# Attention and two feed-forward blocks on one core: zero products of 512 columns, feature rows by transfers, value sums on GpSimd, two heads' values in split halves

## The chip, the core and the metric

One core of a Trainium2 chip runs the whole program. TensorE multiplies, VectorE and ScalarE work on what it leaves in PSUM and on SBUF, GpSimd and SyncE issue most transfers. The metric is the device time of one execution in microseconds, as a median of several runs. One execution is also taken by the hardware profiler, and all rows below come from it.

## The reference

Bucketed attention, then two feed-forward blocks, all in float32. With 2 x 8 heads, 768 positions and 64 features:

```python
q_bits = (np.einsum('bhsd,dk->bhsk', q, proj) > 0)      # 6 bits; the same for k
mask = q_bucket[:, :, :, None] == k_bucket[:, :, None, :]
scores = np.where(mask, scale * q @ k.T, -1e9)
attn = exp(scores - max); attn = attn / (sum + 1e-9)
x = attn @ v                                            # (1536, 512)
h = x @ w_in; g = h * tanh(softplus(h)); x = g @ w_out  # d_ff 2048
h = (x @ w1) * (x @ w2) @ w3; out = h @ w_out2          # d_ff 1024
```

## The kernel before, in words

**A head.** Head u's q and k are loaded (L411), split into a rounded half and the rest for one-pass products (`hlqk`, L400 and L432), transposed on TensorE (L441) and copied to `qb` and `kb` by ScalarE (L447). Products with `psel` (L472) give the projections, and VectorE compares them with zero (L479); the resulting bits are 12 extra feature rows of `qa` and `ka`, whose other 64 rows are copies from `qb` and `kb` (L400; the 12 rows of `ka` are copied at L484). From head 2 on, a further operand `xf` is filled by two transfers on SyncE's queue (L456).

A head has six rows of scores, of 128 positions by 768. A row is four products into a score tile `s` (L499; two such tiles exist, `s_67` and `s_68`, and transposes and projections use them too), a maximum on VectorE (L508) and an exponential on ScalarE into `E` (L511). For each half of three rows, six groups of three transposes (L545) bring `E` to PSUM, a copy takes each to SBUF as `T` (L400, on ScalarE or VectorE), and three groups of two products (L569) multiply `T` with the values `v`. These are full float32 products of 64 output rows, and the trace shows each as two records. The groups end with a copy and an add into `X` (L577, L590). Two more columns of `T`, holding 1/768, yield the mean of the values, which L596 adds up. The row sums' reciprocals go through a transpose (L528) and a transfer to memory.

**Weights.** GpSimd issues the loads (L622). The weights are decoded in one ScalarE and three VectorE instructions (L606, L609, L612, L615), and split into halves where they are used (L661 and L663); L694 to L720 multiply w3 by w_out2 beforehand, which is wprod in the code. The first block of 512 tokens passes the feed-forward part among the later heads (L775, L791, L886), the other two blocks follow from about 523 us on (L775, L1133, L1160, L1188).

**What sets the order.** No loop does. Every piece is a unit with an engine, a cost, a due time and what it reads and writes; `Plan.run` simulates the engines with these costs and the latencies in `LAT`, and lets each engine take whichever unit can start first, the earlier due time deciding. The result is one fixed instruction order for each engine, in which an instruction waits for everything ahead of it. `CFG` holds the numbers that set due times (in rows of scores) and pool sizes. After that, `Plan.fill` puts zero products (L392, results never read) into TensorE's order wherever the plan has a gap in its first 60 us:

```python
n = int((b - a - 0.15) / 0.06)
...
nc.tensor.matmul(t[:, 0:128], lhsT=zr, rhs=zr, start=True, stop=True)
```

Of the kernel before, what the change touches and what calls it, by code (L numbers as in the profile page):

```python
# [26 lines left out]
CFG = {  # L27
    "lag": 1.18,
    "prep": 8.06,
    "wp0": 16.01,  # L30
    "wp1": 51.97,
    "dec0": 47.99,
    "dec1": 88.63,
    "ff0": 56.0,
    "ff1": 102.69,
# [7 lines left out]
    "tc": 22,  # L43
# [39 lines left out]
class Plan:  # L83
    LAT = {"PE": 0.22, "DVE": 0.17, "ACT": 0.17, "POOL": 0.3, "SP": 2.3, "SWAP": 0.0}
# [202 lines left out]
def kernel(  # L287
# [68 lines left out]
    TP = mkpool("T", 7, [128, HS + 2], pa)  # L356
# [7 lines left out]
    VP = mkpool("v", 4, [128, C, D], pa)  # L364
    TM = mkpool("tm", 2, [D, HS + 2], pa)
# [54 lines left out]

    def prep(u, d0, step):
# [5 lines left out]
        for x, (nm, hi, fb) in enumerate((("q", 0, qb), ("k", 1, kb))):  # L427
# [16 lines left out]
            P.op("PE", 6 * 0.082, tr, r=[hl], w=[t], due=d(x + 1), name=f"tq{u}")  # L444
# [8 lines left out]
        if u > 1:  # L453
            xf = Val(XF, "x")
            for sl, fb, nm in ((slice(0, D), qb, "q"), (slice(D, 2 * D), kb, "k")):
                P.op("SP", 0.5, lambda sl=sl, fb=fb: nc.sync.dma_start(  # L456
                    out=xf()[sl].bitcast(F32), in_=fb()[sl].bitcast(F32)), r=[fb], w=[(xf, nm)], due=d(2.5), lat=2.0, name=f"xf{u}")
        P.op(EITHER, (act(S, True), dve2(S)), lambda e: copy(e, qa()[0:D], qb()[0:D]),
             r=[qb], w=[(qa, "x")], due=d(2.2), name=f"fa{u}")
        P.op(EITHER, (act(S, True), dve2(S)), lambda e: copy(e, ka()[0:D], kb()[D:2 * D]),  # L460
             r=[kb], w=[(ka, "x")], due=d(3.2), name=f"fa{u}")
# [16 lines left out]
        def cmp():  # L478
# [5 lines left out]
        P.op("DVE", dve2(S), lambda: nc.vector.tensor_copy(out=ka()[D:KR], in_=qa()[96:96 + 2 * NB]),  # L484
             r=[(qa, "m")], w=[(ka, "m")], due=d(4.6), name=f"km{u}")
# [4 lines left out]
    v_mvs, v_rd = Val(), Val()  # L490
# [25 lines left out]
    def norm(u, due):  # L516
# [3 lines left out]
        def sc():  # L520
# [7 lines left out]
        P.op("PE", 0.16, lambda: nc.tensor.transpose(t()[0:C, 0:128], s()[:, 3], ident), r=[(s, 3)], w=[t],  # L528
             due=due + 0.5, name=f"nt{u}")
# [4 lines left out]
            r=[rt], w=[(v_rd, (u, ))], due=due + 0.7, lat=2.2, name=f"rd{u}")  # L534
# [4 lines left out]
    def unit(u, a, kt, due):  # L539
# [9 lines left out]
        f = et[u, a, kt] = Val(TP, "T")  # L549

        def cp(eng):
            copy(eng, f()[:, 0:HS], t()[:, 0:HS])

        if CFG["tc"] > n0_of(u, a):
            eng, cost = ("ACT",), (act(HS) + 0.02,)
        else:
            eng, cost = EITHER, (act(HS) + 0.02, dve(HS))
        P.op(eng, cost, (lambda: cp("ACT")) if len(eng) == 1 else cp, r=[t], w=[f], due=due + 0.15, name=f"TC{u}.{a}.{kt}")

    def values(u, a, j, due):  # L560
# [4 lines left out]
        n = HS + 2 if a == 0 else HS  # L565

        def mm():
            for x in range(2):
                nc.tensor.matmul(  # L569
                    t()[x * D:(x + 1) * D, 0:n], lhsT=vs[u]()[:, 2 * j + x, :], rhs=fs[x]()[:, 0:n],  # L570
                    start=(j == 0), stop=(j == CH - 1))

        P.op("PE", 0.93, mm, r=fs + [vs[u]], w=[t], due=due, name=f"V{u}.{a}.{j}")
# [671 lines left out]
```

## Time and profile before

| | |
|---|---|
| median of 3 runs | 838.75 us (838.18 to 839.08) |
| the profiled execution | 839.55 us, of which the span from first to last instruction is 837.8 |
| TensorE busy | 823.1 us, 98% of the span |
| VectorE, ScalarE busy | 551.3 and 465.7 us |
| mean granted clock of TensorE | 0.998 |
| moved by the DMA queues | 118.47 MB |

Busy time is the union of an engine's records; records of neighbouring instructions overlap a little, so means by line add to more. Idle time costs only on the engine that the end waits for. The span runs from a head's start-up (to some 40 us) over the attention heads (the last scores at 491 us) to the two later token blocks.

### The profile page before, as it was taken

To read this page: it belongs to the slowest core of one execution; us is meant where nothing else is said; L and a number is where in the kernel's file an instruction comes from. 1 tells how busy PE (TensorE), PEld (TensorE's weight loads), DVE (VectorE), ACT (ScalarE), POOL (GpSimd) and SP (SyncE) were. 2 spreads that over 40 slices of the span, in tenths; PEclk is the share of its full clock that TensorE was granted. 3 is DMA by queue.
4 is the path that set the end of the run, shared out by engine and by line. 5 is a ranking of instruction groups with operands and counts; after the bars stand their busy time and mean duration, and the time that the engine had idled before them with its cause. 6 is when DMAs were issued, how large, how long until landed. Compare 5 with 4: busy or idle time off the path is not lost.

```text
span 837.8 us, 10922 instructions
## 1 busy us (share of the span) xinstructions
PE 823.1 (98%) x4198; PEld 637.1 (76%) x4198; DVE 551.3 (66%) x782; ACT 465.7 (56%) x735; POOL 42.5 (5%) x84
## 2 busy tenths in 40 slices
PE   9999999999989999999999999999999999999998
PEld 9977777777666766767777777888888888888886
DVE  3489878778889899989997566733644334332412
ACT  3379865666879978877675444633343333342311
POOL 3000000000101111111110000000000000000000
PEclk9999999999999999999999999999999999999999
DMA  7514433333956758667662203933212208300001
GB/s 271 222 36 152 139 112 103 111 92 115 286 178 209 256 176 275 243 217 268 217 205 72 83 6 133 407 125 104 79 69 88 102 1 317 110 26 1 1 0 51
DMA packets 40356, 118.47 MB, mean 141 GB/s; under 512 B 4496, under 2 KB 10992, under 8 KB 39280
## 3 DMA queue, kind: packets, MB, share of 16 engines
q1 hardware_dynamic: 27936, 67.31, 24.3%
q0 software_dynamic: 12224, 50.34, 17.5%
q8 instruction: 33, 0.54, 0.3%
q14 instruction: 19, 0.16, 0.1%
q10 hardware_dynamic: 144, 0.13, 0.0%
HBM read 94.37 MB, written 17.87 MB: 134 GB/s over the span
## 4 chain that ended last, share of the span: by engine, by line
PE 78%; DVE 12%; DMA 4%; issue 3%; ACT 3%; SPq 0%; DVEq 0%; ACTq 0%
PE s L1160 11%; PE b L1133 11%; PE s L775 11%; PE b L791 6%; PE b L569 6%; PE b L886 6%; PE b L1188 5%; PE s L499 5%; PE b L545 5%; PE b L711 4%; PE b L392 4%; DMA f<-r_d 3%; DVE st L508 2%; PE s L472 2%; PE b L775 2%
## 5 line engine op out<-in xcount | busy, mean ns | idle before, releaser
L663 DVE TENSOR_TENSOR k<-f,k 128x1024 fp32r<-128x1024 f32 x96 | 116.0, 1219 | 76.4 <-ACT k L661 76.2
L661 ACT CAST k<-f 128x1024 fp32r<-128x1024 f32 x96 | 99.2, 1047 | 20.5 <-DMA f<-keep_wo 7.8
L511 ACT ACTIVATE E<-s,st 128x768 f32<-128x768 f32 x96 | 86.8, 904 | 41.1 <-DVE st L508 40.0
L508 DVE TENSOR_REDUCE st<-s 128x1 f32<-128x768 f32 x96 | 90.9, 951 | 21.6 <-PE s L499 20.9
L400 ACT COPY T<-b 128x384 f32<-128x384 f32 x129 | 60.4, 483 | 60.1 <-PE b L545 59.8
L545 PE MATMUL b<-ident,E 128*128 128x128 f32 x576 | 93.1, 275 | 0.1
L545 PEld LDWEIGHTS b<-ident,E 128*128 128x128 f32 x576 | 71.0, 140 | 28.6 <-issue 9.0
L1160 PE MATMUL s<-k,k 128*128 128x512 f32 x384 | 91.2, 394 | 0.0
L1133 PE MATMUL b<-k,k 128*128 128x512 f32 x384 | 90.3, 393 | 0.0
L775 PE MATMUL s<-k,k 128*128 128x512 f32 x384 | 89.9, 391 | 0.0
L569 PE MATMUL b<-T,v 128*64 128x386 f32 (+1 forms) x384 | 85.2, 515 | 2.7 <-DVE T L400 2.7
L1160 PEld LDWEIGHTS s<-k,k 128*128 128x128 f32 x384 | 72.1, 188 | 16.8
L1133 PEld LDWEIGHTS b<-k,k 128*128 128x128 f32 x384 | 72.1, 188 | 16.5
L775 PEld LDWEIGHTS s<-k,k 128*128 128x128 f32 x384 | 72.1, 188 | 15.9
L791 PE MATMUL b<-k,k 128*128 128x512 f32 x288 | 81.0, 412 | 1.6 <-DVE k L851 1.6
L791 PEld LDWEIGHTS b<-k,k 128*128 128x128 f32 x288 | 51.3, 191 | 22.2 <-issue 9.6
L1111 ACT ACTIVATE f<-s 128x1024 f32<-128x1024 f32 x16 | 16.4, 1027 | 75.1 <-PE s L775 75.1
L1169 DVE TENSOR_TENSOR f<-s,f 128x512 f32<-128x512 f32 x16 | 11.1, 692 | 69.6 <-ACT f L1168 69.6
L499 PE MATMUL s<-kb,qb 128*128 128x384 f32 x192 | 53.2, 358 | 3.0 <-ACT E L511 2.7
L711 PE MATMUL b<-k,k 128*128 128x512 f32 x192 | 55.3, 413 | 0.0
L775 PE MATMUL b<-k,k 128*128 128x512 f32 x192 | 54.7, 410 | 0.5 <-ACT rt L530 0.5
L886 PE MATMUL b<-k,k 128*128 128x512 f32 x192 | 54.9, 411 | 0.0
(113 smaller groups left out, 1169.2 us busy)
## 6 DMA issues: line engine op xcount, KB each, us to landing
k<-in_moe_w_dram POOLq DMA_DIRECT2D x16, 1024.0 KB, 6.8
k<-in_moe_w_out_dram POOLq DMA_DIRECT2D x12, 1024.0 KB, 8.2
f<-keep_wi SPq DMA_DIRECT2D x24, 512.0 KB, 4.5
f<-keep_wo SPq DMA_DIRECT2D x24, 512.0 KB, 3.4
k<-in_moe_w_in_dram POOLq DMA_DIRECT2D x8, 1024.0 KB, 7.4
f<-keep_wa SPq DMA_DIRECT2D x12, 512.0 KB, 5.8
f<-keep_wb SPq DMA_DIRECT2D x12, 512.0 KB, 7.2
f<-wp_d SPq DMA_DIRECT2D x12, 512.0 KB, 3.7
```

The costliest lines, as they stand in the source:

```text
L499: nc.tensor.matmul(t()[:, a, 0:HS], lhsT=l()[0:kk, i * 128:(i + 1) * 128], rhs=r()[0:kk, a * HS:(a + 1) * HS], start=(l is qb), stop=(l is ...
L508: P.op("DVE", 0.868, lambda: nc.vector.tensor_reduce(out=s()[:, 0, i:i + 1], in_=t()[:, :, 0:HS], axis=AX.XY, op=ALU.max, negate=True), r= ...
L545: nc.tensor.transpose(t()[:, ci * 128:(ci + 1) * 128], es[ci]()[:, kt * 128:(kt + 1) * 128], ident)
L569: nc.tensor.matmul(t()[x * D:(x + 1) * D, 0:n], lhsT=vs[u]()[:, 2 * j + x, :], rhs=fs[x]()[:, 0:n], start=(j == 0), stop=(j == CH - 1))
L661: P.op("ACT", act(1024, True), lambda: nc.scalar.copy(out=hl()[:, 0:1024], in_=f()), r=[f], w=[(hl, 0)], due=due, name="hi")
L663: P.op("DVE", dve(1024), lambda: nc.vector.tensor_sub(out=hl()[:, 1024:2048], in0=f(), in1=hl()[:, 0:1024]), r=[f, (hl, 0)], w=[(hl, 1)], ...
L711: nc.tensor.matmul(acc(), lhsT=hv()[:, ws, g_, :], rhs=wview(wo2[g_ // 2], 2)[:, rs, g_ % 2, :], start=(n == 0), stop=(n == 3 * GT - 1))
L775: nc.tensor.matmul(of(), lhsT=wview(w, KD)[:, ws, kk, (f % 2) * 128:(f % 2) * 128 + 128], rhs=kview(xhl[n][kk // 2], xs, kk), start=(m == ...
L791: nc.tensor.matmul(of(), lhsT=l(), rhs=rr(), start=(m == 0), stop=(m == len(ops) - 1))
L886: nc.tensor.matmul(t(), lhsT=wview(w, KD)[:, ws, kk, f2 * 128:f2 * 128 + 128], rhs=kview(x2[kk // 2], xs, kk), start=(kk == 0 and s == 0), ...
L1133: nc.tensor.matmul(t(), lhsT=wview(w, 2)[:, ws, f, dd * 128:(dd + 1) * 128], rhs=gv[:, gs, f, :], start=(j == 0 and f == 0 and s == 0), st ...
L1160: nc.tensor.matmul(t()[:, x, :], lhsT=wview(w, KD)[:, ws, kk, (f % 2) * 128:(f % 2) * 128 + 128], rhs=kview(xx[kk // 2], xs, kk), start=(k ...
```

## The change

Zero products have 512 columns, read the identity `identr` for both operands, and are counted by 0.43 us each in the plan's first 8 us and by 0.235 after. The 64 feature rows of `qa` and `ka` and the 12 bit rows of `ka` come by transfers on SyncE's queue from head 1 on. GpSimd sums the values of each head over six chunks in three adds, and a product with a column of 1/768 (next to the reciprocals' transpose) takes the mean; the two extra columns of `T` and the adds of L596 go. For heads 3 and 4 the values and `T` are split into halves, so that four one-pass products of 384 columns stand for two full ones. The copies of `T` may be VectorE's from the start. And several numbers that the plan orders by are others, the latencies it assumes too. The line numbers of the changed kernel are some 30 higher (L411 is L415, L508 is L535).

```diff
 CFG = {
-    "lag": 1.18,
-    "prep": 8.06,
-    "wp0": 16.01,
+    "lag": 1.92,
+    "prep": 10.06,
+    "wp0": 20.27,
...
+    "fv0": 3,
+    "fv1": 5,
...
-    LAT = {"PE": 0.22, "DVE": 0.17, "ACT": 0.17, "POOL": 0.3, "SP": 2.3, "SWAP": 0.0}
+    LAT = {"PE": 0.22, "DVE": 0.17, "ACT": 0.17, "POOL": 0.3, "SP": 3.2, "SWAP": 0.0}
...
-            n = int((b - a - 0.15) / 0.06)
-            if n < 4:
+            n = int((b - a - 0.1) / (0.43 if a < CFG["cold"] else 0.235))
+            if n < 1:
...
-            nc.tensor.matmul(t[:, 0:128], lhsT=zr, rhs=zr, start=True, stop=True)
+            nc.tensor.matmul(t.rearrange("p (a n) -> p a n", a=4), lhsT=identr, rhs=identr[:, None, :].to_broadcast([128, 4, 128]),
+                             start=True, stop=True)
...
+            nc.gpsimd.tensor_add(out=o, in0=t()[:, 0:3], in1=t()[:, 3:6])
+            nc.gpsimd.tensor_add(out=o[:, 0], in0=o[:, 0], in1=o[:, 1])
+            nc.gpsimd.tensor_add(out=o[:, 0], in0=o[:, 0], in1=o[:, 2])
+
+        P.op("POOL", 1.3, total, r=[t], w=[m], due=u * C, name=f"vs{u}")
...
+    def feature(u, o, to, f, fr, part, due, name):
+
+        r = [(f, "m")] if part == "m" else [f]
+        if u < 1:
+            P.op(EITHER, (act(S, True), dve2(S)), lambda e: copy(e, o()[to], f()[fr]), r=r, w=[(o, part)], due=due, name=name)
+        else:
+            P.op("SP", 0.5, lambda: nc.sync.dma_start(out=o()[to].bitcast(F32), in_=f()[fr].bitcast(F32)),
+                 r=r, w=[(o, part)], due=due, lat=4.5, name=name)
...
-        P.op("DVE", dve2(S), lambda: nc.vector.tensor_copy(out=ka()[D:KR], in_=qa()[96:96 + 2 * NB]),
-             r=[(qa, "m")], w=[(ka, "m")], due=d(4.6), name=f"km{u}")
+        feature(u, ka, slice(D, KR), qa, slice(96, 96 + 2 * NB), "m", d(4.6), f"km{u}")
...
+            nc.tensor.matmul(t()[rows, 256:258], lhsT=vsum[u]()[:, 0], rhs=mean, start=True, stop=True)
...
+        if u in FRV:
+            P.op("DVE", dve(HS), lambda: nc.vector.tensor_sub(out=f[1](), in0=t()[:, 0:HS], in1=f[0]()), r=[t, f[0]],
+                 w=[f[1]], due=due, name=f"TL{u}.{a}.{kt}")
...
+                if u in FRV:
+                    w = vs[u]()[:, kt * 2 * D:(kt + 1) * 2 * D]
+                    ops += [(slice(0, 128), w, fs[x][s], x + s == 0, x + s == 2) for s in range(2)]
+                else:
+                    ops.append((rows, vs[u]()[:, kt], fs[x][0], True, True))
```

**Where the order moves: TensorE's start.** The first rows of TensorE's order before, up to the transposes of head 0's two halves (`hlqk`); `crow` holds the constants that VectorE copies to `ccol`.

```order
L392 MATMUL b_70<-zr 128x128 x25
L966 MATMUL b_69<-ident,crow 128x128 x2
L392 MATMUL b_70<-zr 128x128 x28
L441 MATMUL s_67<-identr,hlqk_102 128x128 x6
L441 MATMUL s_68<-identr,hlqk_103 128x128 x6
L392 MATMUL b_69<-zr 128x128 x6
```

The same place in the changed kernel, where the constants stand in `f_154`:

```order
L395 MATMUL b_70<-identr 128x512 x3
L996 MATMUL b_69<-ident,f_154 128x128 x2
L395 MATMUL b_70<-identr 128x512 x5
L470 MATMUL s_67<-identr,hlqk_95 128x128 x6
L470 MATMUL s_68<-identr,hlqk_96 128x128 x6
L395 MATMUL b_69<-identr 128x512
```

Fifty-three zero products of 128 columns ahead of head 0's first transpose have become eight of 512.

**TensorE among head 0's scores.** Before, from head 0's first row of scores (two rows of the order):

```order
L499 MATMUL s_67<-kb_91,qb_89 128x384 x2
L499 MATMUL s_67<-ka_95,qa_93 128x384 x2
L392 MATMUL b_69<-zr 128x128 x40
L499 MATMUL s_67<-kb_91,qb_89 128x384 x2
L499 MATMUL s_67<-ka_95,qa_93 128x384 x2
L392 MATMUL b_69<-zr 128x128 x40
```

And in the changed kernel, right behind head 0's first row of scores, where head 1's projections (`qb_83`, `kb_85`) come:

```order
L499 MATMUL s_68<-qb_83,psel 128x384
L499 MATMUL s_68<-kb_85,psel 128x384
L395 MATMUL b_69<-identr 128x512 x7
L526 MATMUL s_68<-kb_84,qb_82 128x384 x2
L526 MATMUL s_68<-ka_88,qa_86 128x384 x2
L526 MATMUL s_67<-kb_84,qb_82 128x384 x2
L526 MATMUL s_67<-ka_88,qa_86 128x384 x2
L395 MATMUL b_69<-identr 128x512 x7
```

Each row of scores was followed by 40 zero products and used the tile `s_67` alone; now the second and third row use both tiles with no zero product between them, and seven of 512 columns stand on either side.

**VectorE at heads 3 and 4.** In the changed kernel, ahead of and after a maximum of head 3 (L535), where `k_773` and `f_837` are weights being decoded, and `b` is a PSUM tile with transposed exponentials:

```order
L650 SCALAR_TENSOR_TENSOR f_837<-f_837,k_610 128x1024
L506 TENSOR_SCALAR qa_86<-s_68,ccol 64x768
L589 TENSOR_TENSOR T_888<-b_70,T_881 128x384
L535 TENSOR_REDUCE st_106<-s_67 128x1
L644 TENSOR_SCALAR k_773<-f_868 128x1024
L629 TENSOR_TENSOR k_437<-b_72,tm_101 64x128
L629 TENSOR_TENSOR k_504<-b_72,tm_101 64x256
L404 CAST T_909<-b_69 128x384
L647 SCALAR_TENSOR_TENSOR k_773<-k_773 128x1024
L589 TENSOR_TENSOR T_930<-b_69,T_909 128x384
L589 TENSOR_TENSOR T_935<-b_70,T_921 128x384
```

Before, around two maxima of heads 3 and 4 (L508):

```order
L484 COPY ka_95<-qa_93 12x768
L508 TENSOR_REDUCE st_112<-s_68 128x1
L522 TENSOR_SCALAR st_112<-st_112 128x6
L523 SCALAR_TENSOR_TENSOR st_112<-st_112 128x6
L524 RECIPROCAL st_112<-st_112 128x6
L400 CAST hlqk_102<-rw_98 128x6x64
L432 TENSOR_TENSOR hlqk_102<-rw_98,hlqk_102 128x6x64
L400 COPY qa_94<-qb_90 64x768
L508 TENSOR_REDUCE st_113<-s_68 128x1
L590 TENSOR_TENSOR k_612<-b_69,tm_108 64x384
L596 TENSOR_TENSOR mvs<-b_69,tm_108 64x1
```

Each transposed group of these heads now brings a subtraction (L589) to VectorE, and the copies of feature rows (`qa_94<-qb_90`) and the one-column adds (L596) are gone from it.

## Rows read from the trace of the kernel before

**Rows 1.** The page, busy time of each engine, share of span, instructions.
```profile
PE 823.1 (98%) x4198; PEld 637.1 (76%) x4198; DVE 551.3 (66%) x782; ACT 465.7 (56%) x735; POOL 42.5 (5%) x84
```

**Rows 2.** TensorE by line and shape: count, busy us, mean ns, idle before.
```profile
L499 PE MATMUL s<-kb,qb 128*128 128x384 f32 x192 | 53.2, 358 | 3.0 <-ACT E L511 2.7 <-ACT qb L447 0.2
...
L569 PE MATMUL b<-T,v 128*64 128x384 f32 x192 | 43.8, 518 | 2.7 <-DVE T L400 2.7
...
L392 PE MATMUL b<-zr 128*128 128x128 f32 x272 | 38.4, 305 | 1.1 <-DVE zr L385 1.1
...
L528 PE MATMUL b<-ident,st 128*6 128x128 f32 x16 | 4.4, 273 | 0.0
```

**Rows 3.** TensorE's timeline, 0 to 28 us: start, us, instructions, idle before.
```profile
1.05 5.59 PE L392 MATMUL b<-zr 128*128 128x128 f32 x25 [1.05 <-DVE zr L385]
...
6.75 6.21 PE L392 MATMUL b<-zr 128*128 128x128 f32 x28
...
12.76 1.72 PE L441 MATMUL s<-identr,hlqk 128*128 128x128 f32 x12
...
18.39 0.52 PE L472 MATMUL s<-qb,psel 128*128 128x384 f32 x1
...
18.71 0.52 PE L472 MATMUL s<-kb,psel 128*128 128x384 f32 x1
...
21.83 0.58 PE L499 MATMUL s<-kb,qb 128*128 128x384 f32 x2
...
22.62 4.58 PE L392 MATMUL b<-zr 128*128 128x128 f32 x40
```

**Rows 4.** Timelines of ScalarE and VectorE, from 0 and 150 us.
```profile
2.03 0.30 ACT L386 CAST identr<-ident 128x128 fp32r<-128x128 f32 x1
...
7.13 0.16 DVE L969 COPY ccol<-b 128x2 f32<-128x2 f32 x1 [6.13 <-PE b L966]
...
7.21 0.35 DVE L400 CAST hlqk<-rw 128x384 fp32r<-128x384 f32 x1
...
7.48 1.02 DVE L432 TENSOR_TENSOR hlqk<-rw,hlqk 128x384 fp32r<-128x384 f32 x2
...
153.82 0.96 DVE L508 TENSOR_REDUCE st<-s 128x1 f32<-128x768 f32 x1 [0.85 <-PE s L499]
```

**Rows 5.** Stretch: length, each engine's busy us (instructions), clock, DMA share, GB/s.
```profile
60.00:80.00 20.00, 19.25 (x128) 14.10 (x129) 19.39 (x30) 17.07 (x36) 1.06 (x2) 1.00 0.44 144
```

**Rows 6.** TensorE's waits: us in total, times, longest.
```profile
PE b L569 <- DVE T L400: 2.7, 3, 1.3
...
PE s L499 <- ACT E L511: 2.7, 3, 2.1
```

**Rows 7.** VectorE and ScalarE by line and shape, as rows 2.
```profile
L663 DVE TENSOR_TENSOR k<-f,k 128x1024 fp32r<-128x1024 f32 x96 | 116.0, 1219 | 76.4 <-ACT k L661 76.2
...
L508 DVE TENSOR_REDUCE st<-s 128x1 f32<-128x768 f32 x96 | 90.9, 951 | 21.6 <-PE s L499 20.9
...
L612 DVE SCALAR_TENSOR_TENSOR k<-k 128x1024 int32<-128x1024 int32 x36 | 44.3, 1231 | 0.5
...
L615 DVE SCALAR_TENSOR_TENSOR f<-f,k 128x1024 int32<-128x1024 int32 x36 | 43.8, 1216 | 0.3
...
L400 DVE COPY T<-b 128x384 f32<-128x384 f32 x63 | 34.7, 551 | 16.2 <-PE b L545 12.8 <-ACT tm L577 3.0
...
L609 DVE TENSOR_SCALAR k<-f 128x1024 int32<-128x1024 int32 x36 | 25.1, 699 | 0.4 <-ACT f L606 0.2
...
L479 DVE TENSOR_SCALAR qa<-s,ccol 64x768 fp32r<-64x768 f32 x16 | 17.4, 1086 | 5.0 <-PE s L472 4.7
...
L511 ACT ACTIVATE E<-s,st 128x768 f32<-128x768 f32 x96 | 86.8, 904 | 41.1 <-DVE st L508 40.0
```

**Rows 8.** GpSimd by line, as rows 2.
```profile
L989 POOL CAST psel<-pq 64x6 fp32r<-64x6 f32 x4 | 0.6, 186 | 6.3 <-DVE pq L975 6.3
```

**Rows 9.** The transfers into xf, from issue to landing.
```profile
DMA to landing us min/median/max: 2.5/2.6/5.8
```

More of the change, by code (lines that the diff above doesn't have):

```diff
@@ L456, in prep @@
                 P.op("SP", 0.5, lambda sl=sl, fb=fb: nc.sync.dma_start(
[L457 to L461, printed above, removed]
+                    out=xf()[sl].bitcast(F32), in_=fb()[sl].bitcast(F32)), r=[fb], w=[(xf, nm)], due=d(2.5), lat=4.5, name=f"xf{u}")
+        for f, fb, sl, x in ((qa, qb, slice(0, D), 2.2), (ka, kb, slice(D, 2 * D), 3.2)):
+            feature(u, f, slice(0, D), fb, sl, "x", d(x), f"fa{u}")
         t = Val(SP_, "tq", 1)
@@ L564, in values @@
         fs = [et.pop((u, a, 2 * j + x)) for x in range(2)]
-        n = HS + 2 if a == 0 else HS
         def mm():
+            ops = []
             for x in range(2):
[L569 to L573, printed above, removed]
+                rows = slice(x * D, (x + 1) * D)
+                kt = 2 * j + x
+                if u in FRV:
+                    w = vs[u]()[:, kt * 2 * D:(kt + 1) * 2 * D]
+                    ops += [(slice(0, 128), w, fs[x][s], x + s == 0, x + s == 2) for s in range(2)]
+                else:
+                    ops.append((rows, vs[u]()[:, kt], fs[x][0], True, True))
+            for r, w, f, first, last in ops:
+                nc.tensor.matmul(t()[r, 0:HS], lhsT=w, rhs=f(), start=first and j == 0, stop=last and j == CH - 1)
+        P.op("PE", 0.70 if u in FRV else 0.93, mm, r=[f for fx in fs for f in fx[:1 + (u in FRV)]] + [vs[u]], w=[t],
+             due=due, name=f"V{u}.{a}.{j}")
         if j < CH - 1:
@@ L576, in values @@
         tm = Val(TM, "t")
-        P.op("ACT", act(n), lambda: nc.scalar.copy(out=tm()[:, 0:n], in_=t()[D:2 * D, 0:n]),
+        P.op("ACT", act(HS), lambda: nc.scalar.copy(out=tm(), in_=t()[D:2 * D, 0:HS]),
              r=[t], w=[tm], due=due + 0.3, name=f"VE{u}.{a}")
@@ L594, in values @@
             c = c1
-        if a == 0:
-            P.op("DVE", 0.07, lambda: nc.vector.tensor_add(
-                out=mvs[rows, b * KD + kk:b * KD + kk + 1], in0=t()[0:D, HS:HS + 1], in1=tm()[:, HS:HS + 1]),
-                r=[t, tm], w=[(v_mvs, u)], due=due + 0.5, name=f"mv{u}")
     keep = {}
@@ L622, in rawload @@
         P.op("POOL", 1.0, lambda: nc.gpsimd.dma_start(
-            out=raw().rearrange("p (m n) -> p m n", m=m), in_=src), w=[raw], due=due, lat=8.0, name=nm + "l", after=after)
+            out=raw().rearrange("p (m n) -> p m n", m=m), in_=src), w=[raw], due=due, lat=9.5, name=nm + "l", after=after)
         return raw
@@ L954, in setup @@
         P.op("POOL", 0.2, lambda: nc.gpsimd.memset(psel2.bitcast(F32), 0.0), w=[p2z], due=-9, name="p2z")
-        ones = Val()
-        def one():
-            for t in TP.bufs:
-                nc.gpsimd.memset(t[:, HS:HS + 2], 1.0 / S)
-        P.op("POOL", 1.4, one, w=[ones], due=-8, name="ones")
+        P.op("POOL", 0.1, lambda: nc.gpsimd.memset(mean, 1.0 / S), w=[v_mean], due=-8, name="mean")
         t = Val(BP, "c")
```

80 lines of the change are left out of this document (46 added, 34 removed).

## The prediction

> **What bounds the kernel now.** I read the busy line first: TensorE is busy for 823.1 of 837.8 us [rows 1], so nothing but less work on TensorE, or fewer of its 14.7 idle us, shortens the span. Then TensorE's groups by line [rows 2]: among the real products stands L392, the zero products, 272 of them and 38.4 us. They compute nothing; they stand in TensorE's in-order queue where the planner expects a gap, so they cost whatever the real gap is shorter than they are. The timeline of the start shows how much [rows 3, 4]. Both splits of head 0 (L432) end at 7.48 + 1.02 = 8.50, but the transposes that read them begin at 12.76, behind 28 zero products begun at 6.75. The splits themselves are late in the same way: VectorE's copy of ccol waited 6.13 us for two transposes which stand behind 25 zero products. After S0, the first row of scores at 21.83, 40 zero products run for 4.58 us, though the planner's formula (0.06 us each) meant 2.4. So head 0 is paced by zero products. The 34th row of scores (head 5's fourth, heads from 0) has its maximum taken at 153.82 [rows 4]; the zero products all stand ahead of it.
>
> When they go, the next bound has to be named. VectorE is busy 19.39 of the 20 us from 60 to 80 [rows 5], and TensorE's largest waits are for VectorE's copies of T and for ScalarE's exponentials, which wait for VectorE's maxima [rows 6]. VectorE is what will be waited for.
>
> **Zero products.** The order of the changed kernel has 32 with 512 columns instead of 272 with 128. A price: at the start, 384-column products begin 0.32 us apart (18.39 and 18.71), which is TensorE at 1.2 GHz, so 512 columns take 0.43 there; later zero products come twice as fast (4.58/40 = 0.11 against 5.59/25 = 0.22), which is 2.4 GHz, and 512 columns take 0.21. Nine stand ahead of the first projection: 9 x 0.43 + 23 x 0.21 = 8.7 us. That is 38.4 - 8.7 = 29.7 us less on TensorE, all of it ahead of the 34th maximum. If TensorE never waited in place of them, that maximum would come at about 124 and the span fall to 808. It will wait; so I work out VectorE's time to the same point.
>
> **VectorE up to the sixth maximum.** The zero products now read identr, ready at 2.03 + 0.30 [rows 4]; three take until 3.7, two transposes until 4.0, ccol until 4.5, one cast and two splits (0.35 + 1.02, the other cast being ScalarE's now) until 5.9. Five zero products end at 6.2, so the transposes of head 0 start there instead of at 12.76. From there to the end of head 0's projections took 18.71 + 0.32 - 12.76 = 6.3 us, and to S0 another 2.8; six zero products inside (1.3 us) become one. S0: 6.2 + 6.3 + 2.8 - 0.9 = 14.4. One row of scores then needs 0.8 on TensorE (21.83 to 22.62), a maximum of 0.95 and an exponential of 0.90 [rows 7] with some 0.2 to read out its sum, with some 0.15 from engine to engine: 3.3 us. Both score tiles now alternate (before, s_67 alone did), so a row takes half of that, 1.65; five rows, one comparison (1.09) and half a microsecond give 14.4 + 0.8 + 8.2 + 1.1 = 24.5 for the sixth maximum. I hold this to 3 us either way.
>
> **VectorE from there to the 34th maximum.** I counted its instructions in the order ahead of that maximum, 192, at the means of [rows 7]: 33 maxima 31.3; 10 decodes of three instructions (0.70 + 1.23 + 1.22) 31.5; 21 T copies 11.6; 22 new subtractions T minus its high half, which the trace lacks and which I price as the T copy of the same 384 columns, 12.1; 6 comparisons 6.5; 4 splits of 1024 columns 4.9; 16 splits of a head at 0.51 (1.02/2) 8.2; and 60 small ones at an estimated 0.37, between 0.16 (ccol) and 0.70: 22.2. Together 128.3, less 5% since records overlap (7.13 + 0.16 passes 7.21): 122. The new subtractions alone could lie between 0.35 and 0.70 each, 4 us down or 3 up. Ahead of the sixth maximum stand 31 of these, 15.4 in the same prices. So 106.5 us of VectorE's work lie between. At 95% busy (97% is the 60 to 80 stretch) that is 112 us, and the 34th maximum comes at 24.5 + 112 = 136.6 instead of 153.8: **17 us earlier**. On TensorE the work ahead of it is then the same as before within 1 us (six transposes and two value groups fewer, ten other transposes and three 512-column products more), so this is what is gained. TensorE waits about 13 us on the way, the rest of its 29.7.
>
> **Values in split halves (heads 3 and 4).** Twelve groups of four 384-column products replace twelve that cost 0.91 each (L569, 43.8/48 [rows 2]). A new product costs between 0.16 (half of 0.32) and 0.28 (L499, 53.2/192), so 0.64 to 1.11 a group: 3.2 us less to 2.4 more. I take 0.2 (near L499's own streaming), 1.3 less. The price on VectorE is the 22 subtractions above, 24 in all.
>
> **Means.** Sixteen tiny products replace two columns and 16 small adds on VectorE. Bounds: nothing, and 0.27 each (the record of L528, the nearest [rows 2]); I take 0.1, since records overlap: 1.6 more. The sums on GpSimd run 3 per head beside everything; the nearest row is a 64 x 6 cast of 0.19 [rows 8], so 0.6 a head below, and above perhaps four times that. Queued behind them on GpSimd are the weight loads; a sum waits for its values' load.
>
> **Feature rows by transfers.** 45 more DMAs on SP take 30 half-tile copies and 15 copies of 12 rows off ScalarE and VectorE. The nearest transfer, xf, lands 2.5 to 5.8 us after its issue, 2.6 in the middle [rows 9], where a copy took 0.55. Comparison (1.1), issue (0.5), landing and 0.2 make 4.4 us, 7.6 at worst, from the projections' end to that head's first scores. In the new order TensorE has 7.6 to 13.4 us of other work between the two from head 2 on (3.1 to 12.7 before). I count nothing: that work hides it. Uncovered it is 3 us a head.
>
> **Sum.** 837.8 - 17.2 - 1.3 + 1.6 = 820.9. From the 34th maximum on I leave the waits as they are. The profiled execution took 839.55, 1.75 above its span and 0.8 above the median of 838.75; I take the median's distance, and **forecast 822**.
>
> **A rule weighed.** VectorE is the bound to 136 us, so what slows it counts. The trace has no GpSimd arithmetic beside VectorE's, so nothing in it says whether the sums hold VectorE up. If each held it for its whole length, five heads at 0.6 to 2.4 us would add 3 to 12 us ahead of the 34th maximum; later heads have slack, and the time would be 825 to 834. The Trainium skill (SBUF — State Buffer, Who interferes with whom) says just this: a GpSimd instruction that reads SBUF and a VectorE instruction with two SBUF inputs block each other whole. No row here shows it; nor is every VectorE instruction of that kind (the 33 maxima and the T copies are not), so I put it with the rivals.
>
> **Rivals.**
> (a) VectorE holds less: it stays 97% busy and the small ones are cheaper. Then 24.5 + 103/0.97 = 130.7, 6 us better, 816; with a quicker start 812. Chance 0.14.
> (b) VectorE is held up: 89% busy, as when GpSimd's sums block it, gives 24.5 + 119.7 = 144, a gain of 9.6, so 829, and 834 with a late transfer or two. Chance 0.2.
> (c) The larger zero products do not bring the clock up, and TensorE runs at 1.2 GHz through head 0. Twenty-eight zero products at 0.43 cost 6 us more than at half of it, the scores 2 to 3: the sixth maximum at 31 to 33, time 829. In the trace the low level lasts past 18.71 although TensorE had been busy since 1.05 [rows 3]. So being busy alone did not raise it. The Trainium skill (TensorE: Matmul & The Clock Gate, What's actually happening) has sustained activity release the clock; by busy time alone that would have happened in the first microseconds, and the trace disagrees. Chance 0.1.
> (d) **Slower than before.** SP issues in order, and a feature transfer stands behind value loads and weight loads that wait. If every head's rows of bits land late, TensorE waits at each first row of scores. To eat 19 us over heads 2 to 15 needs 1.35 us a head, in heads with 7.6 us of cover a landing 7.2 us after issue, in those with 12 us over 11; the longest seen is 5.8. It would read 841 to 850. Chance 0.06.
> No change within 0.2% (837.1 to 840.4, about what a measurement of this kernel can tell): 0.02. The forecast itself, 816 to 828: 0.48.
>
> **Range.** 812 to 835 leaves out (d), no change and the far end of (a). Faster 0.92, same 0.02, slower 0.06.
>
> **What the profile will show.** Right: L395 with 32 products under 10 us; head 0's transposes near 6 us; the sixth maximum near 24.5 and the 34th near 136; VectorE at 9 tenths and over from 25 to 130, with TensorE's waits there, some 13 us, released by VectorE and ScalarE; the last 310 us as before. Wrong: first scores of a head waiting for a DMA (d); VectorE's two-input subtractions longer than 0.55 or 1.22 (b); products of 384 columns 0.32 apart after 12 us (c).

## The result, and the profile after

The changed kernel takes 811.85 us in the median of 4 runs (810.17 to 812.81), the kernel before beside it 838.91 (838.18 to 839.9). The ratio is 0.9675, with a 95% interval of 0.9653 to 0.9696: 27 us faster, where 17 were forecast. The time lies 0.15 us below the range's lower end.

The profiled execution has a span of 811.0 us. Its busy line, which answers to [rows 1]:

```profile
PE 797.3 (98%) x3990; PEld 613.3 (76%) x3990; DVE 557.3 (69%) x789; ACT 444.5 (55%) x710; POOL 71.7 (9%) x126
```

TensorE has 25.8 us less work, VectorE 6.0 more. TensorE's groups by line and shape, beside [rows 2]:

```profile
L609 PE MATMUL b<-T,v 128*64 128x384 f32 x336 | 73.3, 515 | 0.2 <-DVE T L404 0.2
...
L609 PE MATMUL b<-T,f 128*128 128x384 f32 x48 | 11.2, 352 | 0.5 <-DVE k L737 0.4
L395 PE MATMUL b<-identr 128*128 128x512 f32 x32 | 10.7, 461 | 2.4 <-ACT identr L389 2.4
...
L499 PE MATMUL s<-xf,psel 128*128 128x384 f32 x28 | 9.6, 341 | 2.2 <-DMA xf<-kb 2.2
L560 PE MATMUL b<-mean,vs 128*64 128x2 f32 x32 | 4.4, 208 | 0.0
```

The zero products (L395) went from 38.4 to 10.7 us of records. The first group of L609 is the unsplit values, the second the split ones. TensorE's start, beside [rows 3]:

```profile
2.38 1.65 PE L395 MATMUL b<-identr 128*128 128x512 f32 x3 [2.38 <-ACT identr L389]
...
6.12 1.15 PE L470 MATMUL s<-identr,hlqk 128*128 128x128 f32 x12
...
8.89 0.41 PE L499 MATMUL s<-qb,psel 128*128 128x384 f32 x1
9.14 0.34 PE L499 MATMUL s<-kb,psel 128*128 128x384 f32 x1
9.32 0.34 PE L499 MATMUL s<-qb,psel 128*128 128x384 f32 x1
...
12.82 0.53 PE L526 MATMUL s<-kb,qb 128*128 128x384 f32 x2
```

Head 0's transposes begin at 6.12 instead of 12.76, and the twelve take 1.15 us instead of 1.72. Its projections come 0.25 us apart once, then 0.18, where before products of this size were still 0.32 apart, the 1.2 GHz level, at 18.7. The trace's clock records begin with full clock, 2.4 GHz, at 5.8 us, those of the trace before at 19.4; what stands ahead of them is read from the spacing. S0 starts at 12.82 instead of 21.83. VectorE's maxima of the first rows and the 34th:

```profile
13.84 0.96 DVE L535 TENSOR_REDUCE st<-s 128x1 f32<-128x768 f32 x1 [0.19 <-PE s L526]
...
16.98 1.82 DVE L535 TENSOR_REDUCE st<-s 128x1 f32<-128x768 f32 x2 [1.06 <-PE s L526]
20.10 2.00 DVE L535 TENSOR_REDUCE st<-s 128x1 f32<-128x768 f32 x2 [1.30 <-PE s L526]
23.41 0.95 DVE L535 TENSOR_REDUCE st<-s 128x1 f32<-128x768 f32 x1
...
130.43 0.94 DVE L535 TENSOR_REDUCE st<-s 128x1 f32<-128x768 f32 x1
```

The sixth maximum comes at 23.41, the 34th at 130.43. Both executions are divided at these two. Of each stretch the columns are its length, then the busy us (and instructions) of TensorE, its weight loads, VectorE, ScalarE and GpSimd, then granted clock, DMA share and GB/s. (The clock column counts the start, where the trace has no clock record, as 1.00.) Before:

```profile
0.00:48.50 48.50, 47.45 (x328) 45.64 (x328) 23.24 (x41) 20.05 (x32) 7.27 (x31) 1.00 0.58 213
48.50:153.80 105.30, 104.13 (x637) 76.67 (x636) 87.72 (x138) 73.83 (x147) 3.42 (x6) 1.00 0.37 111
153.80:837.80 684.00, 671.50 (x3238) 514.81 (x3236) 440.33 (x604) 371.83 (x557) 31.85 (x47) 1.00 0.42 141
```

And after:

```profile
0.00:23.40 23.40, 20.21 (x111) 17.11 (x113) 15.91 (x31) 11.65 (x21) 8.43 (x27) 1.00 0.78 238
23.40:130.40 107.00, 104.73 (x628) 80.78 (x625) 102.79 (x162) 78.95 (x157) 16.82 (x26) 1.00 0.58 184
130.40:811.00 680.60, 672.34 (x3254) 515.37 (x3252) 438.62 (x598) 353.87 (x534) 46.45 (x73) 1.00 0.45 146
```

This is the main reading. Of 26.8 us of span, the first stretch gives 25.1, the second, which I took for VectorE's, takes 1.7 back, and the last gives 3.4. In the second stretch TensorE is busy for 104.73 of 107.00 us: it waited 2.3 us there, not 13.

### The profile page after: what moved, and what is told of

Its sections match the earlier page's. It is cut to its first block, busy times and chain, and to the rows that moved or that the text cites. A ratio compares the mean times of both kernels' runs of the same rounds, so it can differ in the third digit from the quotient of the medians.

```text
span 811.0 us, 10704 instructions
## 1 busy us (share of the span) xinstructions
PE 797.3 (98%) x3990; PEld 613.3 (76%) x3990; DVE 557.3 (69%) x789; ACT 444.5 (55%) x710; POOL 71.7 (9%) x126
## 4 chain that ended last, share of the span: by engine, by line
PE 76%; DVE 15%; DMA 4%; issue 3%; ACT 1%; SPq 0%; POOL 0%; DVEq 0%; POOLq 0%
PE s L1190 11%; PE b L1163 11%; PE s L810 11%; PE b L826 8%; PE b L1218 5%; PE b L609 5%; PE b L810 5%; PE s L526 4%; PE b L580 4%; DVE st L535 4%; PE b L746 4%; PE b L921 3%; DVE k L647 2%; DVE f L650 2%; PE s L499 1%
## 5 line engine op out<-in xcount | busy, mean ns | idle before, releaser
L535 DVE TENSOR_REDUCE st<-s 128x1 f32<-128x768 f32 x96 | 90.8, 948 | 5.8 <-PE s L526 4.4
L580 PEld LDWEIGHTS b<-ident,E 128*128 128x128 f32 x576 | 70.7, 141 | 26.1 <-issue 6.6
L1163 PE MATMUL b<-k,k 128*128 128x512 f32 x384 | 90.1, 392 | 0.0
L826 PE MATMUL b<-k,k 128*128 128x512 f32 x288 | 78.3, 406 | 0.0
L609 PE MATMUL b<-T,v 128*64 128x384 f32 x336 | 73.3, 515 | 0.2 <-DVE T L404 0.2
L1199 DVE TENSOR_TENSOR f<-s,f 128x512 f32<-128x512 f32 x16 | 11.1, 692 | 69.1 <-ACT f L1198 69.1
L526 PE MATMUL s<-kb,qb 128*128 128x384 f32 x192 | 56.3, 374 | 1.3 <-ACT kb L476 0.8
L404 ACT COPY T<-b 128x384 f32<-128x384 f32 x92 | 43.2, 480 | 24.4 <-PE b L580 23.4
L810 PE MATMUL b<-k,k 128*128 128x512 f32 x192 | 54.2, 410 | 0.2 <-DVE k L797 0.2
L921 PE MATMUL b<-k,k 128*128 128x512 f32 x192 | 53.3, 409 | 0.2 <-DVE mvs L404 0.2
L1198 ACT COPY f<-s 128x512 f32<-128x512 f32 x16 | 9.4, 587 | 76.4 <-PE s L1190 76.4
```

The lines of the kernel that those rows point to most:

```text
L526: nc.tensor.matmul(t()[:, a, 0:HS], lhsT=l()[0:kk, i * 128:(i + 1) * 128], rhs=r()[0:kk, a * HS:(a + 1) * HS], start=(l is qb), stop=(l is ...
L535: P.op("DVE", 0.868, lambda: nc.vector.tensor_reduce(out=s()[:, 0, i:i + 1], in_=t()[:, :, 0:HS], axis=AX.XY, op=ALU.max, negate=True), r= ...
L580: nc.tensor.transpose(t()[:, ci * 128:(ci + 1) * 128], es[ci]()[:, kt * 128:(kt + 1) * 128], ident)
L609: nc.tensor.matmul(t()[r, 0:HS], lhsT=w, rhs=f(), start=first and j == 0, stop=last and j == CH - 1)
L810: nc.tensor.matmul(of(), lhsT=wview(w, KD)[:, ws, kk, (f % 2) * 128:(f % 2) * 128 + 128], rhs=kview(xhl[n][kk // 2], xs, kk), start=(m == ...
L826: nc.tensor.matmul(of(), lhsT=l(), rhs=rr(), start=(m == 0), stop=(m == len(ops) - 1))
```

## The experiments

Three theories of the gain: **Z**, the gain is the zero products' time on TensorE; **V**, it is work taken off VectorE (copies, small adds), which was said to set the pace to the 34th maximum; **O**, it is the new order. Behind "Measured" stand the median of four runs and its ratio to the kernel before, run on the same chip; every other number is of the profiled execution.

**1. The changed kernel with the old zero products.**

```diff
-            n = int((b - a - 0.1) / (0.43 if a < CFG["cold"] else 0.235))
-            if n < 1:
+            n = int((b - a - 0.15) / 0.06)
+            if n < 4:
...
-            nc.tensor.matmul(t.rearrange("p (a n) -> p a n", a=4), lhsT=identr, rhs=identr[:, None, :].to_broadcast([128, 4, 128]),
-                             start=True, stop=True)
+            nc.tensor.matmul(t[:, 0:128], lhsT=zr, rhs=zr, start=True, stop=True)
```

> The changed kernel with the zero products of before: 128 columns from a tile of zeros, counted at 0.06 us each, 157 of them in its own order (32 of 512 columns in the changed kernel, 9.8 us by record spacing). Theory Z (the gain is TensorE time that zero products took ahead of the 34th maximum): about 57 stand in the first 8 planned us at 0.22 and 100 later at 0.11, 23.5 us, so 13 us more on TensorE and, less what falls into waits, 819 to 826. Theory V (the gain is work taken off VectorE) and theory O (the gain is the new order): the zero products fall into gaps that are there anyway, 811 to 815.

Measured: 827.68 us, ratio 0.985 (0.9817 to 0.9882); sixth maximum 37.9, 34th 145.2, span 823.7. The median lies above all three ranges, nearest to theory Z's.

**2. The kernel before with the new zero products alone** (the same edit the other way).

> The kernel before with nothing changed but the zero products: 512 columns, read from the identity, counted at 0.43 and 0.235 us; its plan then takes 60 of them instead of 272 of 128. Theory Z: 60 cost about 15 us instead of 38.4; the old order still gives all of head 0's scores one tile, 3.3 us a row, so the sixth maximum comes at about 32 instead of 48.5, and VectorE, whose work ahead of the 34th maximum is smaller here, holds less: 817 to 824. Theories V and O: most of the gain needs the transfers or the order, 830 to 838.

Measured: 821.76 us, ratio 0.9782 (0.9746 to 0.9818); sixth maximum 33.7, 34th 137.9, span 819.0.

**3. The changed kernel without any zero product** (`fill` is not called).

> The changed kernel without any zero product. Theory Z: they now stand in waits, so taking them away gives at most a few us, 807 to 813, if TensorE's clock comes up all the same with head 0's transposes and projections. If the zero products are what raises the clock, 384-column products stay 0.32 us apart well past 10 us, the scores of head 0 come later by 3 to 8 us, and the time is 815 to 822.

Measured: 815.24 us, ratio 0.9714 (0.9677 to 0.9752); 23.4, 130.4, span 811.8. The interval overlaps that of the whole change. The time lies at the lower end of the second range expected, but its reason is not there: nothing moves up to the 34th maximum. In the first stretch TensorE has 5.4 us less to do (14.81 instead of 20.21), and the stretch is as long as with zero products. TensorE's timeline without zero products:

```profile
4.41 1.73 PE L467 MATMUL s<-identr,hlqk 128*128 128x128 f32 x12 [1.55 <-DVE hlqk L458]
7.32 0.97 PE L467 MATMUL s<-identr,hlqk 128*128 128x128 f32 x6 [1.17 <-DVE hlqk L458]
...
9.82 0.52 PE L496 MATMUL s<-kb,psel 128*128 128x384 f32 x1
10.14 0.44 PE L496 MATMUL s<-qb,psel 128*128 128x384 f32 x1
10.42 0.34 PE L496 MATMUL s<-kb,psel 128*128 128x384 f32 x1
```

The spacing falls after 10.1 us, and the clock records begin with full clock at 10.4. So the clock comes up with no zero product ahead of it too, 4.6 us later than with nine.

**4. The old code with the new numbers of `CFG` and the latencies alone.**

```diff
-    "lag": 1.18,
-    "prep": 8.06,
+    "lag": 1.92,
+    "prep": 10.06,
...
-    "tc": 22,
+    "tc": 0,
```

> The kernel before with the new due-time numbers and assumed latencies alone; its zero products stay (128 columns at 0.06 us), its copies stay on VectorE and ScalarE. Theory O: most of the gain is here, 812 to 822. Theory Z: the zero products still cost some 38 us ahead of head 2, 830 to 842. Theory V: no work is taken off VectorE, 834 or more.

Measured: 851.28 us, ratio 1.013 (1.0101 to 1.016); 50.0, 161.9, span 848.6. The numbers alone make the old code slower, by more than theory Z allowed too, so theory O falls in this form. Experiment 2 came out as theory Z said: it holds for 18.8 of 26.8 us. But experiment 1 is 14 us faster than before with the old zero products: something in the new code is worth about as much, and the two overlap.

**5. The changed kernel without the split halves** (theory V's test: VectorE loses 13 us of work where it was said to be the bound).

```diff
-    "fv1": 5,
+    "fv1": 3,
```

> The changed kernel, but heads 3 and 4 are multiplied as all other heads are: no subtractions of T, no split of their values. The order is planned anew. Theory V (between the sixth and the 34th maximum VectorE's work sets the pace): some 13 us of subtractions (24 of 0.544) leave VectorE there, so the 34th maximum comes earlier than 130.4 by what TensorE was idle ahead of it, up to 5 us: 125 to 127, span 805 to 808. Rival T (TensorE's own queue sets the pace, and VectorE is busy because the planner gives it what it has time for): the split made a value group 0.02 us cheaper than an unsplit one (0.78 against 0.80), so nothing moves: 34th maximum at 129.5 to 131.5, span 810 to 813. Rival S (the split pays): the span grows to 814 or more.

Measured: 814.71 us, ratio 0.9689 (0.9669 to 0.9709). The second stretch:

```profile
23.50:131.00 107.50, 105.25 (x623) 75.04 (x620) 94.88 (x147) 76.26 (x147) 15.82 (x26) 1.00 0.57 178
```

VectorE is busy for 94.88 us instead of 102.79, and the stretch is 107.5 us long instead of 107.0. VectorE did not set it. TensorE's 105 us of work do. The span, 813.6, is 0.6 above what rival T gave.

**6. The changed kernel with all feature rows copied.**

```diff
-        if u < 1:
+        if u < NH:
```

> The changed kernel, but all feature rows are copied by ScalarE or VectorE, as before the change, instead of moved by transfers. Theory V: six heads of three copies (0.55, 0.55 and 0.9) come back ahead of the 34th maximum, 12 us of work on two engines, half of it on VectorE: the 34th maximum comes 3 to 6 us later, 133 to 136, span 814 to 817. Rival H (the copies lie beside other work anyway): 34th maximum at 130 to 132, span 810 to 813. Rival D (the transfers were themselves waited for): the span falls below 809.

Measured: 815.46 us, ratio 0.9707 (0.9689 to 0.9725); span 813.2, and the second stretch:

```profile
23.90:132.80 108.90, 102.77 (x616) 78.57 (x612) 104.72 (x170) 83.02 (x156) 16.38 (x27) 1.00 0.48 158
```

Here VectorE has 104.72 us to do, more than TensorE, and TensorE waits 6.1 us. The result lies between the ranges of theory V and rival H. The two engines are within a few microseconds of each other there; whether what VectorE has beyond TensorE's time is what shows is not settled (experiment 13 speaks against it).

**7. GpSimd does the first of its sums three times.**

```diff
-            nc.gpsimd.tensor_add(out=o, in0=t()[:, 0:3], in1=t()[:, 3:6])
+            for _ in range(3):
+                nc.gpsimd.tensor_add(out=o, in0=t()[:, 0:3], in1=t()[:, 3:6])
```

> The changed kernel, but GpSimd does the first of its three sums of a head's values three times over, so 1.7 us more a head (27 us in all, 10 of them ahead of the 34th maximum). If a GpSimd sum holds VectorE up for its whole length: 34th maximum 8 to 10 us later, 138 to 140, span 818 to 822. If it lengthens only the two-input subtractions that it overlaps (in the changed kernel those of line 461 took 596 ns instead of 554): their mean rises to 600 to 650 ns, the 34th maximum moves by under 1.5 us, span 810 to 813.

Measured: 813.38 us, ratio 0.9683 (0.9667 to 0.9698); 131.0, span 811.6. GpSimd is busy for 97.6 us instead of 71.7, and the span stays. The mean of VectorE's subtractions, which was to rise to 600 ns or more, stays too (591 ns against 596).

**8. The old code with the new zero products and the new numbers.**

> The old code with the 512-column zero products and the new numbers of the order and latencies together, without the transfers, the means, the new subtractions. If the two add (zero products alone 18.8 us of span better, numbers alone 10.8 worse): 34th maximum at 146, span 828 to 832. If the new numbers were worse only because they placed more zero products: 34th maximum at 136 to 140, span 815 to 822. Theory V says that the rest down to 811 is work off VectorE and TensorE by the new code, so not under 815.

Measured: 832.92 us, ratio 0.9913 (0.9893 to 0.9934); sixth maximum 35.0, 34th 145.6, span 831.9. The two edits add up; the rest of the code must be worth some 20 us beside these numbers.

So I looked at what the first rows of scores wait for in the kernel with the new zero products alone (experiment 2). They stay on one score tile, 3.1 to 4.4 us apart, as before. TensorE's order before has this, among head 0's scores (the order's rows, not times):

```order
L392 MATMUL b_69<-zr 128x128 x15
L441 MATMUL s_68<-identr,hlqk_102 128x128 x6
L499 MATMUL s_67<-kb_91,qb_89 128x384 x2
```

The middle row is the transposes of head 2's q into the tile `s_68`. Their result is to be copied to a `qb` tile, and there are two: heads 0 and 1 have them. The copy waits for head 0's last row of scores, and `s_68` is held until then. In the profile before, TensorE's row and ScalarE's:

```profile
21.32 0.68 PE L441 MATMUL s<-identr,hlqk 128*128 128x128 f32 x6
...
48.13 0.81 ACT L447 ACTIVATE qb<-s 128x768 fp32r<-128x768 f32 x1 [0.48 <-PE s L499]
```

From 22.0 to 48.1 us one of two score tiles held data that nobody could fetch. The changed kernel has one line against that, which the lines of the diff ahead of the prediction do not show: the transposes also write `(fb, "t")`, so the planner gives them no place before the feature tile is free. Call it the claim. **Theory H**: the claim, with the zero products, is the gain. **Rival N**: the early rows are quick for another reason.

**9. The changed kernel without the claim.**

```diff
-            P.op("PE", 6 * 0.082, tr, r=[hl], w=[t, (fb, "t")], due=d(x + 1), name=f"tq{u}")
+            P.op("PE", 6 * 0.082, tr, r=[hl], w=[t], due=d(x + 1), name=f"tq{u}")
```

> The changed kernel without one word of it: the transposes of a head's q and k no longer claim the feature tile (qb or kb) that they are for, so the planner may place them while that tile is still in use. Theory H (a held score tile): head 2's first transposes then go into one of the two score tiles and stay there until head 0's qb is free, so the first rows of scores share one tile, 3 to 4 us apart instead of 1.6. Then S0 stays near 13.8, the sixth maximum comes at 32 to 35 instead of 23.4, the 34th at 138 to 141, span 818 to 822. Rival N (the early rows are quick because of the new numbers and of what else the code dropped): sixth maximum at 23 to 24.5, 34th at 130 to 132, span 810 to 814.

Measured: 862.45 us, ratio 1.028 (1.0251 to 1.031). Without this one word the change is slower than the kernel before. VectorE's maxima, and ScalarE's copy of head 2's q:

```profile
14.21 0.96 DVE L535 TENSOR_REDUCE st<-s 128x1 f32<-128x768 f32 x1
17.33 0.96 DVE L535 TENSOR_REDUCE st<-s 128x1 f32<-128x768 f32 x1 [2.16 <-PE s L526]
...
31.86 0.81 ACT L476 ACTIVATE qb<-s 128x768 fp32r<-128x768 f32 x1
32.55 0.95 DVE L535 TENSOR_REDUCE st<-s 128x1 f32<-128x768 f32 x1
```

The rows are 3.1 us and more apart, and the sixth maximum stands at 32.55, as expected. The loss beyond it I had not expected; the second stretch:

```profile
32.60:187.10 154.50, 133.37 (x744) 105.09 (x744) 115.57 (x180) 85.04 (x163) 15.10 (x27) 0.96 0.41 132
```

It takes 154.5 us instead of 107. I took the time from the end of each head's q transposes to the start of their copy out of the trace: before it is 26.1 us for head 2 and at most 5 for any other. Here it is 19.1 for head 2 and then 32.1, 30.3, 23.9, 21.9 and 23.5 for heads 3 to 7. In the changed kernel it is 1.6 at most. So the claim's absence costs the more there: one of two score tiles is held for most of that stretch. Why these later heads are held so long only with the rest of the new code is open (with the new numbers in the old code, experiment 4, it is 25.2 for head 2 and 4.8 at most for any other). Not all of the loss need be the tile itself. The plan also places 91 zero products instead of 32:

```profile
L395 PE MATMUL b<-identr 128*128 128x512 f32 x91 | 26.7, 434 | 2.4 <-ACT identr L389 2.4
```

And the granted clock was at half for 3.4 us from 55.3, behind a wait of 3.88 us, and for 10.2 us from 86.0, in a wait of 7.05. No run separates the three.

**10. The kernel before with the claim and the new zero products alone.**

> The kernel before with two edits alone: the 512-column zero products, and the claim of the feature tile by the transposes. Its numbers of the order, its copies, its means and its unsplit values stay. Theory H: S0 near 15.5, sixth maximum at 24 to 26, 34th at 129 to 133, span 809 to 815: with these two the gain is complete, and transfers, means, split and numbers come to 3 us or less together. Rival N: 33.7, 137.9 and 819, as with the zero products alone.

Measured: 815.72 us, ratio 0.973 (0.9702 to 0.9758); 24.4, 131.8, span 813.8.

**11. The kernel before with the claim alone.**

> The kernel before with the claim alone, its 128-column zero products kept. Theory H: sixth maximum at 36 to 40 instead of 48.5 (as the changed kernel with the old zero products, 37.9), 34th at 143 to 147, span 823 to 829. Rival N: 48.5, 153.8 and 838, as before.

Measured: 827.55 us, ratio 0.9865 (0.9845 to 0.9885); 37.0, 144.1, span 826.6. Theory H stands: two small edits bring 2.7 of 3.25%.

How the claim works is in the rows. With the new zero products alone (experiment 2), TensorE's second row of scores waits for the exponential that frees the one tile, and a row takes 3.12 us:

```profile
17.52 0.62 PE L498 MATMUL s<-kb,qb 128*128 128x384 f32 x2 [1.22 <-ACT E L510]
...
18.61 0.96 DVE L507 TENSOR_REDUCE st<-s 128x1 f32<-128x768 f32 x1 [2.16 <-PE s L498]
21.73 0.96 DVE L507 TENSOR_REDUCE st<-s 128x1 f32<-128x768 f32 x1 [2.16 <-PE s L498]
```

With the claim beside them (experiment 10) the same 3.12 us hold two rows:

```profile
17.19 1.82 DVE L507 TENSOR_REDUCE st<-s 128x1 f32<-128x768 f32 x2 [0.46 <-PE s L498]
20.31 0.96 DVE L507 TENSOR_REDUCE st<-s 128x1 f32<-128x768 f32 x1 [1.30 <-PE s L498]
```

On TensorE the claim shows as fewer zero products: 165 instead of 272 of the old ones, 34 instead of 60 of the new. TensorE's busy time falls by 11.1 us with the old (823.1 to 812.0) and 4.8 with the new (800.8 to 796.0), nearly the whole of the 11.2 and 5.2 us of span. What the claim is worth beside no zero product at all was not run.

The last two ask where the other half per cent is. **12. Claim, new zero products and new numbers in the old code.**

> The old code with the claim, the 512-column zero products and the new numbers of the order and latencies: all of the change but transfers, means and split halves. The new numbers made the old code slower both times that it had no claim (1.3% alone, 1.3% beside the zero products). Theory H (there the early order decided, and it is mended by the claim): sixth maximum at 23.5 to 25, 34th at 130 to 134, span 809 to 813, so the numbers are what is left between 813.8 (claim and zero products) and 811.0 (the whole change). Rival L (the numbers cost by themselves): span 818 to 826, and the transfers, means and split have to win that back.

Measured: 816.31 us, ratio 0.9732 (0.9707 to 0.9758); 23.6, 132.1, span 815.4. With the claim these numbers neither cost nor bring anything that can be told. (Two assumed latencies, of `xf` and of the reciprocals' reading, and the buffer counts of `T` and `v` are not among them, here and in experiments 4 and 8, so the expectation's "all of the change but" is a little too wide.) The span lies between those of the two theories, so they do not bring the last 4 us.

**13. The changed kernel with copies and without split halves.**

> The changed kernel with both its feature transfers and its split halves undone: claim, zero products, numbers and the means by the small product remain. Each alone cost about 2 us of span (813.2 and 813.6 against 811.0). If they are independent: 815 to 817. If VectorE's time is what both stand for (the copies give it work, the split's absence takes 13 us from it), they cancel: the stretch from the sixth to the 34th maximum, 108.9 us with copies alone, falls back to 107 to 108, and the span is 811 to 814.

Measured: 815.98 us, ratio 0.9726 (0.9696 to 0.9757); 34th maximum 134.3, span 815.7. They do not cancel. The second stretch:

```profile
24.10:134.30 110.20, 106.24 (x622) 74.72 (x619) 99.90 (x156) 81.66 (x152) 16.95 (x27) 1.00 0.48 161
```

VectorE has 5 us less to do in it than with the copies alone, less than TensorE, and the stretch is 1.3 us longer. Each undone step costs some 2 us of span, both 4.7. So transfers and split halves together are about the last half per cent (the ratio intervals just touch), though either alone is hardly more than the runs can tell. By what they bring it is open.

| kernel | zero products | sixth | to the 34th | from there on | span | ratio |
|---|---|---|---|---|---|---|
| before | 272 | 48.5 | 105.3 | 684.0 | 837.8 | 1 |
| claim | 165 | 37.0 | 107.1 | 682.5 | 826.6 | 0.9865 |
| new zero products | 60 | 33.7 | 104.2 | 681.1 | 819.0 | 0.9782 |
| claim, new zero products | 34 | 24.4 | 107.4 | 682.0 | 813.8 | 0.973 |
| the whole change | 32 | 23.4 | 107.0 | 680.6 | 811.0 | 0.9675 |
| it without the claim | 91 | 32.6 | 154.5 | 670.5 | 857.6 | 1.028 |

## Why the prediction was right and wrong, step by step

**What bounds the kernel.** "Nothing but less work on TensorE, or fewer of its 14.7 idle us" was right, and I left it in the next paragraph for VectorE. TensorE's busy time fell by 25.8 us and its idle time by 1.0, from 14.7 to 13.7: that is the whole gain of 26.8.

**Zero products.** Right in kind and size: forecast 8.7 us, in records 10.7, from start to start 9.8. Ahead of the 34th maximum TensorE's busy time fell from 151.6 to 124.9 (the sums of the stretches above), 26.6 us; the forecast for the zero products by themselves was 29.7, since it took starts (8.7) from records (38.4); from start to start they went from 36.4 to 9.8, the same 26.6. Rival (c) fell: full clock is on record from 5.8 us. With the old zero products (experiment 1) TensorE is busy from 1 us on, and its projections are still 0.32 apart at 21 us. So the old ones both took the place and did not raise the clock, as the rows of before had shown. The Trainium skill (TensorE: Matmul & The Clock Gate, What's actually happening) has activity release the throttle. By busy records alone the runs here disagree: the kernel without zero products, with gaps of 1.55 and 1.17 us, reached 2.4 GHz 11 us sooner than the one that had no gap.

**VectorE up to the sixth maximum.** Right: forecast 24.5, measured 23.41. S0 came at 12.82 instead of 14.4 (its terms were read where TensorE still ran at 1.2 GHz), the five rows took half a microsecond more than forecast, and these partly cancel. But the text gave the whole of it to the zero products. The halving of a row's time to 1.65 us, which it took from the order ("both score tiles now alternate"), is the claim's doing: without the claim the sixth maximum stands at 32.6, so 9.2 of these 25.1 us hang on it. I saw that one tile had been out of use, and did not ask what held it.

**VectorE from there to the 34th maximum.** This step failed. I made 112 us of it, from 106.5 us of VectorE's work at 95% busy, and gained 17.2 at its end; it took 107.0, and the gain there was 23.4. VectorE's work was 102.8, so the count was 3.7 too high. The error behind it is the larger one: I divided VectorE's work by a busy share as if VectorE set the pace. Experiment 5 took 8 us from VectorE in this stretch and it did not shorten. TensorE's own work there, 104 to 105 us before and after, sets it, and that I had noted ("the same as before within 1 us") and not used: the sixth maximum at 24.5 plus the old stretch of 105.3 gives 129.8, against a measured 130.4. "TensorE waits about 13 us on the way" was 2.3. [Rows 5] misled me: VectorE busy for 19.39 of 20 us is one stretch, and TensorE's 19.25 stands beside it. Over the whole old stretch from the sixth to the 34th maximum VectorE was busy for 87.72 of 105.30 us, 83%, and TensorE for 104.13, 99%.

**Values in split halves.** Forecast 1.3 us less. From record start to record start a group took 0.82 us before, 0.80 unsplit and 0.78 split after; the price of 0.91 came from overlapping records. Alone undone it costs nothing that the runs can tell; together with the copies, 4.7 us of span.

**Means.** Forecast 1.6 us. The 32 records hold 3.4 us of TensorE from start to start, 0.2 a product instead of 0.1; so 1.8 more. The transpose just ahead of each also holds TensorE for 0.20 us instead of 0.11, some 1.4 more. Neither is seen in the sum.

**Feature rows.** Counted as nothing. Undone alone they cost about 2 us of span (ratio 0.9707 against 0.9675, intervals that overlap a little): a small gain, whose way is open (experiment 13). Rival (d), late transfers, showed only in the older transfer into `xf`, which TensorE waited 2.23 us for up to 192.17; the granted clock was 0.50, 1.2 GHz, for the 3.4 us from 193.5 on. With the feature rows copied (experiment 6) the wait was 0.6 and the clock stayed up.

**"From the 34th maximum on I leave the waits as they are."** Also wrong, by 3.4 us: TensorE's work is 0.8 us more there and its idle time 8.3 instead of 12.5. The zero products alone, whose order there has not one edit, show 2.9 of it (681.1). In that trace the granted clock stays full there; in the trace before it is 0.50 for 3.4 us from 370.9 on, behind a wait of 1.56 us, which is an estimated 1.7 us of the 2.9. The changed kernel has a fall of the same length, behind `xf`, so in it the 3.4 us have another source, which is not settled.

**Rivals.** (a) came out in time (130.7, and 812 with a quicker start) for a reason that was not its own. (b) fell: with three times the first sum the 34th maximum came 0.5 us later, nearly all of it ahead of the sixth. The forecast missed by 9.9 us of span (820.9 against 811.0): 1.1 in the start, 5.1 in the second stretch, 3.7 after it, where 0.3 more was forecast and 3.4 less came.

## What to carry to other kernels

When an engine has been busy for 98% of the span, first predict with its own work alone, and take another engine for the bound only where rows show the first one idle for it, over the whole stretch and not in one part of it; here VectorE was 97% busy in the 20 us that were read and 83% in the 105 us that counted. When an order shows that a buffer is in use alone, look for what holds the other: a producer that fills a shared tile before its consumer's target is free holds it for as long as that target is taken. Read a diff for edits of a word in what a step claims; here one decided whether the change was faster or slower.

## What the runs showed of the hardware

A zero product does not bring the clock up by being there: with 128-column ones TensorE was busy from 1 us on, and full clock came at 19.4 us (19.4 to 21.4 in the four kernels that have them); with 512-column ones it came at 5.8 (5.6 to 8.4 in ten kernels), and with none at all at 10.4. The two kinds differ in operands too (zeros and the identity), and no run tells columns and operands apart.

GpSimd's sums and VectorE's subtractions with two inputs from SBUF hold each other up, but little. In the changed kernel, two of GpSimd's first sums and the subtractions that began during them:

```profile
122.09 0.63 POOL L428 TENSOR_TENSOR vs<-v 128x192 f32<-128x192 f32 x1 [24.57 <-PE b L560]
122.30 0.84 DVE L461 TENSOR_TENSOR hlqk<-rw,hlqk 128x384 fp32r<-128x384 f32 x1
...
327.21 0.61 POOL L428 TENSOR_TENSOR vs<-v 128x192 f32<-128x192 f32 x1
327.34 0.91 DVE L461 TENSOR_TENSOR hlqk<-rw,hlqk 128x384 fp32r<-128x384 f32 x1
```

The sums end at 122.72 and 327.82, the subtractions 0.42 and 0.43 us after that, whenever they began, and so do the other five that began during a sum (0.41 to 0.42); one that overlaps no sum takes 0.55. They end as if they had stood still, but for their first eighth of a microsecond, until the sum was done. The Trainium skill (SBUF — State Buffer, Who interferes with whom) has two such instructions contend for one exclusive pair of ports, and issue order decide which of them blocks. The trace agrees: the later one waits. It does so the other way round too, where two first sums that began during a subtraction took 0.80 and 0.78 us; those that began first took some 0.6. What it costs VectorE depends on the number of meetings: ten of the 32 subtractions overlap a sum and take 700 ns in the mean, the other 22 take 549, which is 1.5 us for all of them.
